# Loads of 8 KB per partition in a retention and soft-MoE kernel: one transfer per input step, weight tiles in pairs, and separate tile pools

## The chip, the cores and the metric

The kernel runs on one core of a Trainium2 chip. A core has TensorE (matmuls, and the weight loads that run beside them), VectorE (DVE), ScalarE (ACT), GpSimd (POOL) and SyncE (SP), which here issues every transfer, and 16 DMA engines that move data between HBM and the core's SBUF. The metric is the device time of one execution in microseconds; the time of the kernel before is the median of three runs.

## The reference

Retention attention over 4 batches, 8 heads, 768 positions and heads of 64, then a soft mixture of experts over all 3072 tokens. All data are float32.

```python
def _attn_ref(q, k, v):
    gamma = 1.0 - 2.0 ** (-5.0 - np.arange(H))
    for t in range(S):
        state = gamma * state + np.einsum('bhd,bhe->bhde', k[:, :, t], v[:, :, t])
        y[:, :, t] = scale * np.einsum('bhd,bhde->bhe', q[:, :, t], state)

def _moe_ref(x, phi, w1, w2):          # x: 3072 x 512, phi: 512 x 32
    logits = x @ phi
    d = softmax(logits, axis=0)
    slot_input = (d.T @ x).reshape(E, S_per_e, D)      # 8 experts, 4 slots each
    for e in range(E):                                 # w1: 512 x 1024, w2: 1024 x 512 per expert
        slot_out[e] = np.maximum(slot_input[e] @ w1[e], 0.0) @ w2[e]
    return softmax(logits, axis=1) @ slot_out
```

The second softmax over tokens needs all tokens, so no expert can start before the last token has been seen. All of w1 and w2 (32 MB) and q, k, v (k in two layouts) are read once, and 6.3 MB are written.

## The kernel before

*Retention.* The tokens are worked in 24 steps of 128 (6 per batch). Step i loads two tiles of 128 partitions by 1024 floats (4 KB per partition, 512 KB): load_kq brings k and q transposed, load_vk brings v and k in natural layout (the sixth step of a batch loads only v, 256 KB), and GpSimd scales v in place (L169). On TensorE, in this order: scores (L182), which VectorE masks (L187) into a tile A; natural (L234), which transposes the step's output before; the state's part (L202) and the scores' part (L207) of attend, scaled by VectorE into a tile x; and state (L226), copied by ScalarE. After each fourth step come logits (L245), and in the next group's first steps dispatch_p and dispatch_u (L278, L287) and combine_weights (L303).

*Experts.* After step 23 the softmaxes are closed, and hidden(g, k) multiplies the slots with w1 for expert group g (four experts each) and quarter k of the model width (L445): four weight tiles of 512 KB per call, each used in both halves of the call. hidden_t transposes the result. Then three output blocks of 256, 128 and 128 columns: 64 matmuls each with w2 (L537), group 0 first and then group 1; finish adds up the experts (L504), splits the result, and multiplies it with the combine weights (L519). VectorE and ScalarE copy each half into an output tile (L522, L525), which is written out by a transfer of 512 KB (L523). The result matmuls of a block are interleaved with the next block's matmuls. split_c and transpose_c prepare the combine weights.

*What sets the order.* TensorE runs in the order of the code. The other engines are ordered by the framework's scheduler. SyncE issues all transfers one after the other; it cannot go past one whose slot is not free. There are eight completion semaphores for transfers, used in turn, so a transfer is issued only when the one eight places ahead of it has landed.

*Tiles.* Every tile that is not small comes from one ring of 48 slots of 4 KB per partition (slot()): weights, kq and vk tiles, A, x, the combine weights, outputs.

*Weights.* load_weights(n) issues the next n tiles of a list of 64: w1 for group 0, quarters 0 to 3, then group 1, then w2 block by block. 34 tiles are spread over the 23 steps from the first (NPRE), the last two steps and the closing of the softmaxes ask for TAIL = 2, 2, 1 and 2 more, and the calls of hidden for four each.

Of the kernel before, what the change touches and what calls it, by code (L numbers as in the profile page):

```python
# [17 lines left out]
C = 128  # L18
# [6 lines left out]
NE = 8  # L25
# [52 lines left out]
def retention_soft_moe_kernel(  # L78
    ctx: ExitStack,
    tc: tile.TileContext,  # L80
    kq_in: bass.AP,
    vk_in: bass.AP,
    phi: bass.AP,
    w1: bass.AP,
    w2: bass.AP,
# [37 lines left out]
    w1t, w2t, w2n = {}, {}, [0]  # L123
    weights = [("w1", 4 * g + j, k) for g in range(2) for k in range(NK) for j in range(4)]
    for cb, (_, w) in enumerate(BLOCKS):
        for g in range(2):
            if w == 64:
                weights += [("w2", 4 * g + 2 * j, cb) for j in range(2)]
            else:
                weights += [("w2", 4 * g + j, cb) for _ in range(NFC // FPS[w]) for j in range(4)]  # L130

    def load_weights(n):
        for _ in range(n):
            if not weights:
                return
            which, e, k = weights.pop(0)
            t = slot()
            if which == "w1":
                nc.sync.dma_start(t, w1[e, k * 128:(k + 1) * 128, :])
                w1t[e, k] = t  # L140
            else:
                n = 1024 if BLOCKS[k][1] == 64 else FPS[BLOCKS[k][1]] * BLOCKS[k][1]
                nc.sync.dma_start(t[:, 0:n], w2[w2n[0]:w2n[0] + 128 * n].rearrange("(p n) -> p n", n=n))
                w2n[0] += 128 * n
                if BLOCKS[k][1] == 64:
                    w2t[e, k], w2t[e + 1, k] = [t[:, 0:512]], [t[:, 512:1024]]
                else:
                    w2t.setdefault((e, k), []).append(t)
# [3 lines left out]
    def load_kq(i):  # L152
        t = slot()
        nc.sync.dma_start(t, kq_in[i])
        st[i] = dict(kT=t[:, 0:512].rearrange("p (g t) -> p g t", t=C),
                     qT=t[:, 512:1024].rearrange("p (g t) -> p g t", t=C))

    def load_vk(i):
        t = slot()
        v = t[:, 0:512].rearrange("p (h e) -> p h e", e=D)  # L160
        st[i].update(v=v, kn=t[:, 512:1024].rearrange("p (h e) -> p h e", e=D))
        if i % NC == NC - 1:
            nc.sync.dma_start(t[:, 0:512], vk_in[i, :, 0:512])
        elif i == 0:
            nc.sync.dma_start(t[:, 0:512], vk_in[i, :, 0:512])
            nc.sync.dma_start(t[:, 512:1024], vk_in[i, :, 512:1024])
        else:
            nc.sync.dma_start(t, vk_in[i])
        nc.gpsimd.tensor_tensor(v, v, vsc[:, i % NC, :].unsqueeze(2).broadcast_to([128, H, D]), ALU.mult)  # L169

    def scores(i):
# [12 lines left out]
        A = s["A"] = slot().rearrange("p (r g t) -> p r g t", r=2, t=C)  # L184
# [133 lines left out]
    def split_c(q):  # L318
        c4s[q] = slot().rearrange("p (i r h s) -> p i r h s", r=2, h=2, s=NSLOT)
# [3 lines left out]
        nc.vector.tensor_tensor(c4r[:, :, :, 1, :], cq, c4s[q][:, :, :, 0, :], ALU.subtract)  # L323
        c4T[q] = slot()
# [12 lines left out]
    load_kq(0)  # L337
# [6 lines left out]
    load_vk(0)  # L344
    load_kq(1)
    nc.sync.dma_start(kt[:, K_FIRST:], consts[:, K_FIRST:])
    load_vk(1)
# [11 lines left out]
    for i in range(NSTEP):  # L359
# [21 lines left out]
        if i == NSTEP - 3:  # L381
            split_c(0)
        if i == NSTEP - 2:
            split_c(1)
# [6 lines left out]
        if last:  # L391
            logits(NGRP - 1)
        elif i % GRP == GRP - 1:
            logits_mm(i // GRP, range(GRP))
            logits(i // GRP)

# [68 lines left out]
    for k in range(NK):  # L465
        hidden(0, k)
        load_weights(HLOAD if k == 0 else 4)
        if k == 0:
            combine_weights(NGRP - 1)
        if k == 0:  # L470
            hT = [slot().rearrange("p (f e s) -> p f e s", e=NE, s=NSLOT) for _ in range(2)]
# [7 lines left out]
    load_weights(4)  # L479
    hidden(1, 1)  # L480
    hidden_t(0)
    load_weights(4)
# [4 lines left out]
    load_weights(4)  # L487
# [67 lines left out]
def lay_out(q, k, v, moe_phi, moe_w1, moe_w2):  # L555
# [44 lines left out]
```

## Time and profile before

| | |
|---|---|
| median of three runs | 169.55 us (169.42 to 169.83) |
| profiled execution | 170.2 us, of which the span of instructions 168.4 us |
| TensorE's granted clock, mean | 0.997 |
| busy in the span | DVE 56%, ACT 25%, POOL 18% |
| transfers | 128 by the program; 64.62 MB, mean 384 GB/s |
| HBM | 57.96 MB read, 6.29 MB written |

In the profile PE stands for TensorE's matmuls and PEld for its weight loads. The page cuts the span into 40 slices of 4.2 us and gives for each the busy share in tenths and the rate of the DMA engines. A row of instructions names its line in the kernel, the tile written and the tiles read, and the count. In the chain and in timelines the first column is the start and the second the length in us; in rows of waits stand the total, the number of times and the longest; in groups of instructions the busy time and the mean in ns, and then the idle time ahead of them with what ended it. A row of a stretch has its length, then busy time and instructions of PE, PEld, DVE, ACT and POOL, then the granted clock, the share of the DMA engines and their GB/s.

### The profile page before, as it was taken

The numbers are of one execution on the slowest core, as the hardware profiler recorded it, in microseconds if no ns is written. First come the engines' busy times: TensorE is split into PE (matmuls) and PEld (weight loads), VectorE is DVE, ScalarE is ACT, GpSimd is POOL, SyncE is SP. The second block draws the span as 40 slices with busy tenths as digits, with TensorE's granted clock in tenths as the row PEclk, the third lists the DMA queues.
The fourth block names the chain that finished last, engine by engine and source line by source line (L and its number), as shares of the span: only waits on it lengthen the run. The fifth ranks groups of instructions, "written<-read, shape, count | busy, mean of one in ns | idle before, by whom it ended". The sixth has DMA issues, their size and how long they took to land.

```text
span 168.4 us, 5648 instructions
## 1 busy us (share of the span) xinstructions
PE 153.6 (91%) x2370; PEld 109.6 (65%) x2370; DVE 93.6 (56%) x299; ACT 42.0 (25%) x104; POOL 30.5 (18%) x40
## 2 busy tenths in 40 slices
PE   8699779999999999999989799999999999999940
PEld 2577667687868786888678578867432546666620
DVE  0576445596677876694777566984223121355550
ACT  3022213232423141323212232315202030043330
POOL 0252222230304122232223221300050000000000
PEclk9999999999999999999999999999999999999998
DMA  6999999999999999999999999999999999969966
GB/s 185 324 416 411 408 402 415 401 410 406 410 407 406 407 409 406 408 409 404 407 407 411 405 409 406 403 384 367 378 312 404 415 412 406 412 263 397 384 266 263
DMA packets 18458, 64.62 MB, mean 384 GB/s; under 512 B 2048, under 2 KB 2432, under 8 KB 18432
## 3 DMA queue, kind: packets, MB, share of 16 engines
q1 hardware_dynamic: 18432, 64.26, 97.4%
q8 instruction: 19, 0.31, 0.8%
q14 instruction: 7, 0.06, 0.1%
HBM read 57.96 MB, written 6.29 MB: 381 GB/s over the span
## 4 chain that ended last, share of the span: by engine, by line
PE 50%; DMA 40%; DVE 3%; SPq 2%; issue 1%; DVEq 0%
DMA r<-in_kq_dram 18%; DMA r<-in_w_dram 18%; PE sc L537 9%; PE sc L182 6%; PE y L445 4%; PE y L207 4%; DMA r<-in_vk_dram 4%; PE xp L234 3%; PE sm L245 3%; PE y L202 3%; PE xp L445 2%; PE S L445 2%; PE sm L287 2%; PE S L226 2%; PE sm L519 2%; PE sm L331 1%
## 5 line engine op out<-in xcount | busy, mean ns | idle before, releaser
L187 DVE TENSOR_TENSOR r<-sc,kt 128x256 f32<-128x256 f32 x94 | 33.3, 417 | 17.1 <-PE sc L182 16.1
L169 POOL TENSOR_TENSOR r<-r,kt 128x512 f32<-128x512 f32 x24 | 25.1, 1044 | 75.5 <-DMA r<-in_vk_dram 51.1
L213 DVE SCALAR_TENSOR_TENSOR r<-y,kt,ysc 128x128 f32<-128x128 f32 x96 | 27.7, 343 | 9.6 <-PE y L207 6.7
L182 PE MATMUL sc<-r 64*128 64x128 f32 x376 | 27.4, 284 | 4.4 <-DMA r<-in_kq_dram 4.1
L207 PE MATMUL y<-r 128*64 128x128 f32 x384 | 27.3, 280 | 2.6 <-POOL r L169 2.4
L182 PEld LDWEIGHTS sc<-r 64*128 64x128 f32 x376 | 23.1, 187 | 7.3 <-issue 4.0
L207 PEld LDWEIGHTS y<-r 128*64 128x64 f32 x384 | 21.3, 136 | 7.3 <-POOL r L169 3.8
L235 ACT COPY r<-xp 128x512 f32<-128x512 f32 x23 | 13.5, 586 | 42.9 <-PE xp L234 33.3
L234 PE MATMUL xp<-kt,r 128*128 128x128 f32 x96 | 16.5, 287 | 0.1
L537 PE MATMUL sc<-r 128*32 128x128 f32 (+1 forms) x384 | 15.9, 310 | 0.0
L234 PEld LDWEIGHTS xp<-kt,r 128*128 128x128 f32 x96 | 10.6, 141 | 7.0 <-DVE r L187 3.4
L537 PEld LDWEIGHTS sc<-r 128*32 128x32 f32 x384 | 10.6, 110 | 6.0 <-issue 2.9
L228 ACT COPY sst<-S 128x256 f32<-128x256 f32 x20 | 7.5, 373 | 27.6 <-PE S L226 27.5
L202 PE MATMUL y<-r,sst 64*64 64x128 f32 x320 | 13.3, 282 | 0.0
L226 PE MATMUL S<-r 128*64 128x64 f32 x320 | 13.1, 222 | 0.0
L226 PEld LDWEIGHTS S<-r 128*64 128x64 f32 x320 | 12.3, 138 | 0.0
L202 PEld LDWEIGHTS y<-r,sst 64*64 64x64 f32 x320 | 8.5, 132 | 3.3 <-issue 2.1
L445 PE MATMUL y<-r,siT 128*32 128x512 f32 x64 | 8.2, 597 | 0.0
L245 PE MATMUL sm<-r,phis 128*32 128x128 f32 x192 | 7.3, 276 | 0.0
L245 PEld LDWEIGHTS sm<-r,phis 128*32 128x32 f32 x192 | 5.4, 109 | 1.4 <-issue 1.0
L313 POOL TENSOR_TENSOR cnat<-cnat,cz 128x128 f32<-128x128 f32 x6 | 2.4, 401 | 17.5 <-DVE cz L312 14.5
L287 PE MATMUL sm<-r,p 128*32 128x512 f32 x40 | 5.3, 605 | 0.0
(112 smaller groups left out, 124.2 us busy)
## 6 DMA issues: line engine op xcount, KB each, us to landing
r<-in_w_dram SPq DMA_DIRECT2D x64, 512.0 KB, 10.1
r<-in_kq_dram SPq DMA_DIRECT2D x24, 512.0 KB, 10.1
r<-in_vk_dram SPq DMA_DIRECT2D x19, 512.0 KB, 10.1
out_dram<-r SPq DMA_DIRECT2D x12, 512.0 KB, 4.3
r<-in_vk_dram SPq DMA_DIRECT2D x6, 256.0 KB, 9.6
kt<-in_consts_dram SPq DMA_DIRECT2D x1, 136.0 KB, 3.1
kt<-in_consts_dram SPq DMA_DIRECT2D x1, 78.0 KB, 5.6
phis<-in_phi_dram SPq DMA_DIRECT2D x1, 64.0 KB, 6.2
```

Source lines behind the costliest of these rows:

```text
L169: nc.gpsimd.tensor_tensor(v, v, vsc[:, i % NC, :].unsqueeze(2).broadcast_to([128, H, D]), ALU.mult)
L182: nc.tensor.matmul(sc[g // 2][r][:, g % 2, :], s["kT"][sl, g, :], s["qT"][sl, g, :], start=True, stop=True)
L187: nc.vector.tensor_tensor(A[:, r, 2 * hf:2 * hf + 2], sc[hf][r], mask.unsqueeze(1).broadcast_to([128, 2, C]), ALU.mult)
L202: nc.tensor.matmul(y[b][o:o + D, gl, :], sst[sl, g, :], s["qT"][sl, g, :], start=(gl == 0), stop=False, skip_group_check=True)
L207: nc.tensor.matmul(y[g // 2][o:o + D, g % 2, :], s["v"][:, 2 * g + r, :], s["A"][:, r, g, :], start=(c == 0 and g % 2 == 0), stop=True, sk ...
L213: nc.vector.scalar_tensor_tensor(yT[:, g, :], y[g // 2][:, g % 2, :], ybs[:, c, g:g + 1], ysc[:, g, :], ALU.mult, ALU.mult)
L226: nc.tensor.matmul(S_[r * D:(r + 1) * D, g, :], s["kn"][:, 2 * g + r, :], s["v"][:, 2 * g + r, :], start=(c == 0 and g == 0), stop=True, s ...
L234: nc.tensor.transpose(xp[:, g * 128:(g + 1) * 128], s["yT"][:, g, :], ident)
L235: (nc.vector.tensor_copy if i == NSTEP - 1 else nc.scalar.copy)(s["xn"], xp)
L245: nc.tensor.matmul(q["ltp"][32 * j:32 * j + 32, :], phis[:, p, :], st[GRP * g + j]["yT"][:, p, :], start=(p == 0), stop=(p == NPAIR - 1), ...
L445: nc.tensor.matmul(hp[g][half][32 * j:32 * j + 32, :], siT[:, k, :], w1t[4 * g + j, k][:, half * 512:(half + 1) * 512], start=(k == 0), st ...
L537: nc.tensor.matmul(op[32 * j:32 * j + 32, :w], hT[fc // 4][:, fc % 4, 4 * g + j, :], t[:, f * w:(f + 1) * w], start=(g == 0 and fc == 0), ...
```

## The change

Inputs and weights are laid out in memory so that one row of a transfer is 8 KB: x_in holds kq and vk of a step side by side, w_in holds the tiles of two experts side by side. One transfer then moves 1 MB. The amount of data and the arithmetic are the same.

- load_in replaces load_kq and load_vk: one transfer of 1 MB (768 KB in a batch's last step), issued behind state(i). Steps 0 and 1 still come in parts, as before.
- load_weights(n) issues pairs. The ring holds 17 pairs (8 KB slots), and the eighteenth pair goes as two transfers of 512 KB into two slots of the x pool.
- The one ring of 48 slots becomes four pools: the ring (17 of 8 KB), inputs (3 of 8 KB), A (2 of 4 KB), x (6 of 4 KB; outputs and other results too): 192 KB per partition, as before. The combine weights' tiles come from the input pool.
- TAIL becomes 0, 0, 1, 0 and each call in the hidden layer asks for two pairs.
- split_c(0) moves from step 21 to step 22, split_c(1) from step 22 to behind the loop.

```diff
-TAIL = (2, 2, 1, 2)
-HLOAD = 4
+TAIL = (0, 0, 1, 0)
+HLOAD = 2
-NPRE = 34
+NPRE = 17
-NRING = 48
+NRING = 17
+NIN = 3
+NX = 6
...
     ring = ctx.enter_context(tc.tile_pool(name="ring", bufs=NRING))
+    inp = ctx.enter_context(tc.tile_pool(name="inp", bufs=NIN))
+    apool = ctx.enter_context(tc.tile_pool(name="apool", bufs=2))
+    xpool = ctx.enter_context(tc.tile_pool(name="xpool", bufs=NX))
...
     def slot():
-        return ring.tile([128, 1024], F32, name="r", tag="r")
+        return xpool.tile([128, 1024], F32, name="x", tag="x")
+    def a_slot():
+        return apool.tile([128, 1024], F32, name="a", tag="a")
+    def in_slot():
+        return inp.tile([128, 2048], F32, name="in", tag="in")
...
-            t = slot()
-            if which == "w1":
-                nc.sync.dma_start(t, w1[e, k * 128:(k + 1) * 128, :])
-                w1t[e, k] = t
+            src = w_in[wn[0]]
+            wn[0] += 1
+            if nld[0] == NRING:
+                t = [slot(), slot()]
+                for h in range(2):
+                    nc.sync.dma_start(t[h], src[:, 1024 * h:1024 * h + 1024])
             else:
...
+                a = ring.tile([128, 2048], F32, name="r", tag="r")
+                nc.sync.dma_start(a, src)
+                t = [a[:, 0:1024], a[:, 1024:2048]]
+            nld[0] += 1
...
+    def load_in(i, part=None):
+        if part != 1:
+            t = in_slot()
...
+        end = 1536 if i % NC == NC - 1 else 2048
+        if part is None:
+            nc.sync.dma_start(t[:, 0:end], x_in[i, :, 0:end])
...
         attend(i)
-        if i + 2 < NSTEP:
-            load_kq(i + 2)
         state(i)
         if i + 2 < NSTEP:
-            load_vk(i + 2)
+            load_in(i + 2)
         else:
             load_weights(TAIL[i - NSTEP + 2])
...
-        if i == NSTEP - 3:
+        if i == NSTEP - 2:
             split_c(0)
-        if i == NSTEP - 2:
-            split_c(1)
...
     for k in range(NK):
         hidden(0, k)
-        load_weights(HLOAD if k == 0 else 4)
+        load_weights(HLOAD)
...
-    load_weights(4)
+    load_weights(2)
```

Two places of SyncE's program show what moves. First, the loads after the program's first eight transfers; in_kq_dram and in_vk_dram are the inputs, in_w_dram the weights, r a slot of the ring, DMAHW the completion of an earlier transfer. Before:

```order
L139 DMA r<-in_w_dram 128x1024 [waits DMAHW0_49]
L154 DMA r<-in_kq_dram 128x1024 [waits DMAHW1_49]
L168 DMA r<-in_vk_dram 128x1024 [waits DMAHW2_49]
L139 DMA r<-in_w_dram 128x1024 [waits DMAHW3_49]
L154 DMA r<-in_kq_dram 128x1024 [waits DMAHW4_49]
L168 DMA r<-in_vk_dram 128x1024 [waits DMAHW5_49]
L139 DMA r<-in_w_dram 128x1024 [waits DMAHW6_49]
L139 DMA r<-in_w_dram 128x1024 [waits DMAHW7_49]
```

And in the changed kernel (in_x_dram holds the inputs, in is a slot of the input pool):

```order
L174 DMA in<-in_x_dram 128x2048 [waits DMAHW0_49]
L152 DMA r<-in_w_dram 128x2048 [waits DMAHW1_49]
L174 DMA in<-in_x_dram 128x2048 [waits DMAHW2_49,DMAHW3_49,PE_49,Pool_49]
L152 DMA r<-in_w_dram 128x2048
L174 DMA in<-in_x_dram 128x2048 [waits DMAHW4_49,DMAHW6_49,PE_49,Pool_49]
L174 DMA in<-in_x_dram 128x1536 [waits DMAHW0_49,DMAHW5_49,PE_49,Pool_49]
L152 DMA r<-in_w_dram 128x2048
```

Input 2 now comes ahead of the first weights, and from input 3 on each input's load waits for TensorE and GpSimd to be done with the slot it takes.

Second, the end of the inputs and the weights behind them. Before, the last input's two transfers are followed by weight tiles, each of which waits for the eighth transfer ahead and for a slot that some earlier work of TensorE, VectorE, ScalarE or GpSimd leaves:

```order
L154 DMA r<-in_kq_dram 128x1024 [waits DMAHW2_49,DVE_49,PE_49]
L163 DMA r<-in_vk_dram 128x512 [waits DMAHW3_49,PE_49,Pool_49]
L143 DMA r<-in_w_dram 128x1024 [waits DMAHW4_49,PE_49,Pool_49]
L143 DMA r<-in_w_dram 128x1024 [waits DMAHW5_49,PE_49,Activation_49]
L143 DMA r<-in_w_dram 128x1024 [waits DMAHW6_49,PE_49,Activation_49]
L143 DMA r<-in_w_dram 128x1024 [waits DMAHW7_49,DVE_49,PE_49]
L143 DMA r<-in_w_dram 128x1024 [waits DMAHW0_49,PE_49,Pool_49]
```

In the changed kernel:

```order
L174 DMA in<-in_x_dram 128x1536 [waits DMAHW0_49,DMAHW5_49,PE_49,Pool_49]
L152 DMA r<-in_w_dram 128x2048
L149 DMA x<-in_w_dram 128x1024 [waits DVE_49,DMAHW7_49,PE_49,Activation_49]
L149 DMA x<-in_w_dram 128x1024 [waits DVE_49,PE_49,Activation_49]
L152 DMA r<-in_w_dram 128x2048 [waits DMAHW1_49,PE_49]
L152 DMA r<-in_w_dram 128x2048 [waits DMAHW2_49,PE_49]
L152 DMA r<-in_w_dram 128x2048 [waits DMAHW3_49,PE_49]
```

Behind the last input stand the seventeenth pair, which takes the ring's last unused slot, the eighteenth in x slots, and then pairs that take the slots of the first pairs of w1, in turn; those are read by hidden(0, 0), hidden(0, 1) and so on. The 12 output transfers stand behind the last pair on SyncE in both kernels.

More of the change, by code (lines that the diff above doesn't have):

```diff
@@ L80, in retention_soft_moe_kernel @@
     tc: tile.TileContext,
[L81 to L82 removed]
+    x_in: bass.AP,
     phi: bass.AP,
[L84 to L85 removed]
+    w_in: bass.AP,
     consts: bass.AP,
@@ L120, in retention_soft_moe_kernel @@
     ybs = kt[:, K_YB:K_YB + 24].rearrange("p (c g) -> p c g", g=NPAIR)
-    w1t, w2t, w2n = {}, {}, [0]
-    weights = [("w1", 4 * g + j, k) for g in range(2) for k in range(NK) for j in range(4)]
+    w1t, w2t, wn, nld = {}, {}, [0], [0]
+    weights = [("w1", 4 * g + 2 * j, k) for g in range(2) for k in range(NK) for j in range(2)]
     for cb, (_, w) in enumerate(BLOCKS):
         for g in range(2):
[L127 to L130, printed above, removed]
+            weights += [("w2", 4 * g + 2 * j, cb) for _ in range(NFC // FPS[w]) for j in range(2)]
     def load_weights(n):
@@ new lines, in load_weights @@
+            wn[0] += 1
[3 more added lines that the diff above has]
+                    nc.sync.dma_start(t[h], src[:, 1024 * h:1024 * h + 1024])
+            else:
+                a = ring.tile([128, 2048], F32, name="r", tag="r")
+                nc.sync.dma_start(a, src)
+                t = [a[:, 0:1024], a[:, 1024:2048]]
+            nld[0] += 1
+            for h in range(2):
+                if which == "w1":
+                    w1t[e + h, k] = t[h]
@@ L147, in load_weights @@
                 else:
-                    w2t.setdefault((e, k), []).append(t)
+                    w2t.setdefault((e + h, k), []).append(t[h])
     st = {}
[L152 to L163, printed above, removed]
+    def load_in(i, part=None):
+        if part != 1:
+            t = in_slot()
+            st[i] = dict(t=t, kT=t[:, 0:512].rearrange("p (g t) -> p g t", t=C),
+                         qT=t[:, 512:1024].rearrange("p (g t) -> p g t", t=C),
+                         v=t[:, 1024:1536].rearrange("p (h e) -> p h e", e=D),
+                         kn=t[:, 1536:2048].rearrange("p (h e) -> p h e", e=D))
+        t = st[i]["t"]
+        end = 1536 if i % NC == NC - 1 else 2048
+        if part is None:
+            nc.sync.dma_start(t[:, 0:end], x_in[i, :, 0:end])
+        elif part == 0:
+            nc.sync.dma_start(t[:, 0:1024], x_in[i, :, 0:1024])
+            return
@@ L183, in scores @@
                                  start=True, stop=True)
-        A = s["A"] = slot().rearrange("p (r g t) -> p r g t", r=2, t=C)
+        A = s["A"] = a_slot().rearrange("p (r g t) -> p r g t", r=2, t=C)
         for hf in range(2):
@@ L318, in split_c @@
     def split_c(q):
-        c4s[q] = slot().rearrange("p (i r h s) -> p i r h s", r=2, h=2, s=NSLOT)
+        t = in_slot()
+        c4s[q] = t[:, 0:1024].rearrange("p (i r h s) -> p i r h s", r=2, h=2, s=NSLOT)
         c4r = c4s[q].bitcast(F32R)
@@ L323, in split_c @@
         nc.vector.tensor_tensor(c4r[:, :, :, 1, :], cq, c4s[q][:, :, :, 0, :], ALU.subtract)
-        c4T[q] = slot()
+        c4T[q] = t[:, 1024:2048]
     c4p = {}
@@ L343, in retention_soft_moe_kernel @@
                             .broadcast_to([128, NPAIR, 16, 8]), ALU.mult)
-    load_vk(0)
-    load_kq(1)
+    load_in(0, 1)
+    load_in(1, 0)
     nc.sync.dma_start(kt[:, K_FIRST:], consts[:, K_FIRST:])
-    load_vk(1)
+    load_in(1, 1)
     nc.sync.dma_start(phis, phi)
@@ L395, in retention_soft_moe_kernel @@
             logits(i // GRP)
+    split_c(1)
     transpose_c(0, 0, "S")
@@ L470, in retention_soft_moe_kernel @@
         if k == 0:
-            hT = [slot().rearrange("p (f e s) -> p f e s", e=NE, s=NSLOT) for _ in range(2)]
+            hT = [a_slot().rearrange("p (f e s) -> p f e s", e=NE, s=NSLOT) for _ in range(2)]
             for t in hT:
```

34 lines of the change are left out of this document (13 added, 21 removed).

## Prediction

> **What bounds the kernel now.** I read the page first (busy times, the 40 slices, the queues), then the chain, the waits, the timelines of SyncE and TensorE, and the stretches around the end of the retention steps.
>
> ```profile
> PE 153.6 (91%) x2370; PEld 109.6 (65%) x2370; DVE 93.6 (56%) x299; ACT 42.0 (25%) x104; POOL 30.5 (18%) x40
> DMA  6999999999999999999999999999999999969966
> GB/s 185 324 416 411 408 402 415 401 410 406 410 407 406 407 409 406 408 409 404 407 407 411 405 409 406 403 384 367 378 312 404 415 412 406 412 263 397 384 266 263
> q1 hardware_dynamic: 18432, 64.26, 97.4%
> ```
>
> Two resources are full at once. The 16 DMA engines work for 97.4% of the span at about 407 GB/s, and TensorE is busy for 91%. So time in which the DMA engines have nothing to do is lost, and a faster DMA pays only where TensorE waits for it. Where it waits, the waits (in total, times, longest) and TensorE's timeline tell (the bracket is the idle time ahead of a row):
>
> ```profile
> PE sc L182 <- DMA r<-in_kq_dram: 4.1, 5, 1.2
> ...
> 17.89 1.16 PE L182 MATMUL sc<-r 64*128 64x128 f32 x16 [1.12 <-DMA r<-in_kq_dram]
> 23.02 1.16 PE L182 MATMUL sc<-r 64*128 64x128 f32 x16 [1.25 <-DMA r<-in_kq_dram]
> 40.28 1.16 PE L182 MATMUL sc<-r 64*128 64x128 f32 x16 [0.39 <-DMA r<-in_kq_dram]
> 75.74 1.16 PE L182 MATMUL sc<-r 64*128 64x128 f32 x16 [0.19 <-DMA r<-in_kq_dram]
> 87.62 1.09 PE L207 MATMUL y<-r 128*64 128x128 f32 x16 [0.52 <-POOL r L169]
> 94.16 1.16 PE L182 MATMUL sc<-r 64*128 64x128 f32 x16 [1.13 <-DMA r<-in_kq_dram]
> 107.83 1.16 PE L182 MATMUL sc<-r 64*128 64x128 f32 x16
> ```
>
> The row at 23.02 is the scores of step 4, that at 107.83 of step 23. Between them TensorE waits 0.39 + 0.19 + 0.52 + 1.13 = 2.2 us for inputs (the POOL row is the scaling of v, itself behind a load). That is what faster inputs can give after step 4. The chain shows the rest of the program: from 94 us on it names TensorE alone, so weights arrive in time there.
>
> ```profile
> 119.32 1.00 PE xp L445 x8
> 120.31 0.86 PE y L445 x8
> ...
> 155.17 0.43 PE y L519
> ...
> 156.06 0.79 PE sc L537 x24
> ```
>
> 119.32 is the first hidden-layer piece, hidden(0, 0), called T0 below. The row at 156.06 is a piece of output block 2; by the count of matmuls the block's second half, the first user of the last weights, begins in it, at about 156.3. The one at 155.17 is the first result matmul of block 1.
>
> How the queue lives shows in SyncE's timeline and in the times to landing:
>
> ```profile
> 4.01 0.99 SPq L348 DMA_DIRECT2D phis<-in_phi_dram  x1
> ...
> 53.31 0.33 SPq L168 DMA_DIRECT2D r<-in_vk_dram  x1
> 53.97 1.61 SPq L139 DMA_DIRECT2D r<-in_w_dram  x2
> ...
> 96.66 0.33 SPq L154 DMA_DIRECT2D r<-in_kq_dram  x1
> 97.93 0.33 SPq L163 DMA_DIRECT2D r<-in_vk_dram  x1
> 99.22 40.59 SPq L143 DMA_DIRECT2D r<-in_w_dram  x32
> ...
> 111.98 27.83 SPq L143 DMA_DIRECT2D r<-in_w_dram  x24
> 148.52 15.36 SPq L523 DMA_DIRECT2D out_dram<-r  x12
> DMA to landing us min/median/max: 3.2/10.1/11.4
> ...
> phis<-in_phi_dram SPq DMA_DIRECT2D x1, 64.0 KB, 6.2
> SPq L596 <- DMA out_dram<-r: 3.5, 3, 1.2
> out_dram<-r SPq DMA_DIRECT2D x12, 512.0 KB, 4.3
> L523 SPq DMA_DIRECT2D out_dram<-r x12: 332/332/827, 148.5 to 163.4; - x12
> ```
>
> A transfer is issued when the one eight places ahead has landed, so the spacing of issues is the time of one landing: 512 KB take 1.28 us (96.66, 97.93, 99.22), and a step's 256 KB of values alone take 0.66 us (53.31 to 53.97). Eight of them make the 10.1 us to landing. The line of landings is that of the kq loads; its least, 3.2 us, is the first load of the program, alone in the queue: 1.28 us of data and 1.9 us around it.
>
> **The change, part by part.**
>
> *Rows of 8 KB.* No row of the trace moves 8 KB per partition for data. From the two spacings: a fixed part f and d per 256 KB give f + 2d = 1.28 and f + d = 0.66, so d = 0.62, f = 0.04, and 1 MB in one transfer is f + 4d = 2.52 us against 2 x 1.28 = 2.56 now. The spacings are good to about 0.03, so f lies between 0 and 0.10 and 1 MB between 2.46 and 2.56. I take 2.52. The Trainium skill (DMA: Bandwidth & Descriptors, section "Where 436 GB/s comes from") gives the ports into SBUF 435 GB/s at most; the slices of 401 to 416 agree, and by that ceiling 1 MB could not take less than 2.41 us, an estimate from the page, which would take 1.5 us off the sum below (14 loads by 0.11) and leave its sign.
>
> *SyncE issues 75 transfers instead of 128.* At 0.33 us each, spaced by 1.28, SyncE is not what limits; I count nothing.
>
> *Start.* The first eight transfers are the same up to phis, which lands at 4.01 + 6.2 = 10.2 us. Then the queue holds input 2, a pair, input 3, a pair, input 4: 5 x 2.52 = 12.6, so input 4 lands at 22.8 and step 4 starts at 23.0 as now. The waits up to there stay; kq no longer comes ahead of vk, which is in this count.
>
> *Inputs in three slots.* The load of input i+2 now waits until state(i-1) and the scaling of v have released a slot, with the next pair queued behind it on SyncE. It is requested two steps ahead of its use, and a step is (107.83 - 23.02 - 2.2) / 19 = 4.35 us of TensorE. At worst it takes 1.9 + 2.52 + 2.52 (a pair ahead) = 6.9 of 8.7 us, so the wait is hidden; without that slack every step would pay the difference. Over the phase the engines move inputs 5 to 23 (15 whole, 4 of 768 KB, so 18) and 14 pairs: 32 x 2.52 = 80.6, input 23 at 103.4; TensorE wants it at 23.0 + 82.6 = 105.6. The margin is 2.2 us in 83, so nearly all 2.2 us of waits go; I take 2.0 (ends: 0, if the margin is eaten, and 2.2). T0 moves to 117.3. The scaling of v (1.04 us a step) ends behind the scores and transposes of the step, 1.16 + 0.66 us, and stays hidden.
>
> ```profile
> L169 POOL TENSOR_TENSOR r<-r,kt 128x512 f32<-128x512 f32 x24 | 25.1, 1044 | 75.5 <-DMA r<-in_vk_dram 51.1
> L323 DVE TENSOR_TENSOR r<-cnat,r 128x512 fp32r<-128x512 f32 x3 | 2.1, 685 | 0.0
> 118.00:123.00 5.00, 5.00 (x45) 2.18 (x48) 1.31 (x5) 1.27 (x3) 0.00 (x0) 1.00 0.98 355
> 153.00:158.00 5.00, 5.00 (x100) 3.47 (x101) 2.78 (x6) 1.82 (x5) 0.00 (x0) 1.00 1.01 397
> ```
>
> *split_c moves* by a step. The two halves on VectorE (0.7 us and less each) still stand in the last two steps; one now stands ahead of a step's masks. Between -0.7 and +0.7, one such piece hidden or exposed; I take 0, since one of them stood there before.
>
> *Separate pools, the part that decides.* Today one ring of 48 slots serves all, and as inputs end, their slots take weights: after the last input (97.93) SyncE has issued 8 weight tiles by 111.98 (32 less 24), and the row from 118 to 123 us shows the DMA engines still 98% busy, at 355 GB/s. In the changed kernel the 17 pairs of the ring are full with the hidden layer's weights and one pair of the second layer; one more pair goes into two x slots. With input 23 at 103.4 and these two pairs, the last load lands at about 103.4 + 5.1 = 108.5. The next one waits for the release of a pair by hidden(0, 0), whose two halves end at 117.3 + 1.00 + 0.86 = 119.2, and its data follow the latency. About 11 us of DMA time are lost, where today some 4 MB are moved. Then 14 pairs remain, 14 x 2.52 = 35.3 us, released faster than they are moved (two per 1.86 us). The 12 output transfers stand behind them in the same queue. The three last outputs of today land 1.2 us apart (waits of the last row of the program: at most 1.2); between that and 1.28 I take 1.25, 15.0 us for 12. From 163.4 + 4.3 = 167.7 to the span's end 168.4 it is 0.7 us.
>
> *Sum:* 119.2 + 1.9 + 35.3 = 156.4 for the last weights, + 15.0 = 171.4 for the last output, + 0.7 = 172.1. Against 168.4 that is 3.7 us more. The profiled execution took 170.2 (its span and 1.8 us around it), 0.65 above the median of 169.55; I add the difference to the median: 173.3.
>
> **The rivals.**
>
> *Outputs move beside loads* (ends on the other side: no change). If writing to HBM took nothing from reading, the outputs would not stand behind the weights, and only the landing of the last pair would count. Block 2's second half starts 156.3 - 119.3 = 37.0 after T0, which would be 154.3; the pair lands at 156.4, so TensorE loses 2.1 and has gained 2.0: 168.5, a time of 169.7. It decides when more than 3.7 of the 15 us overlap. Against it: 153 to 158 us is nearly output alone and fills the engines to 1.01 at 397 GB/s, and no slice exceeds 416. 0.05.
>
> *A large transfer is much cheaper* (faster). To come out even, 14 loads must win 3.7 us, 0.26 each: 1 MB in 2.26 us. That needs a fixed part of 0.30 per transfer, where the spacings show 0.04; the first load's 1.9 us besides data is hidden with eight in flight. By this mechanism a fixed part of 0.4 would give 2.16 us, a sum of 167.1 and a time of 168.3. The Trainium skill (DMA: Bandwidth & Descriptors, section "Bandwidth") has this as a rule that speaks for the change, to batch to 1 MB and more, with 341 GB/s at 1 MB and 425 at 16 MB. Here queued loads of 512 KB already run at 400 and more, so the trace does not agree that the size costs much. The chance is 0.05.
>
> *8 KB rows save nothing.* At 2.56 us, and 1.28 for an output, the margin of the inputs shrinks to 23.0 + 81.9 = 104.9 against 105.6, and perhaps half of the waits stay (1.1 of gain, T0 at 118.2): 118.2 + 1.9 + 1.9 + 35.8 + 15.4 + 0.7 = 173.9, a time of 175.1. The two spacings are too rough to exclude it. 0.23.
>
> *Six x slots hold up the end.* Block 1's output tiles need slots that block 0's outputs free, and those land only behind the weights, the first at 157.7. Today 7.8 us lie between the end of block 1's first result matmul (155.6) and the last output's issue, then 4.3 to landing: 157.7 + 12.1 = 169.8, under the 171.4 of the queue by 1.6. Copies that wait in line on VectorE and ScalarE and hold TensorE up by 3 us would add 1.4: 174.7. 0.10.
>
> **How the numbers follow.** The forecast as summed has 0.52; 0.05 stays for mixtures between it and today's time, 0.02 of it within 0.3%. Up to the bounds of the costs: 0 gained, 2.56 and 1.28 give 119.3 + 1.9 + 1.9 + 35.8 + 15.4 + 0.7 = 175.0, a time of 176.2; 2.2 gained, 2.46 and 1.2 give 117.1 + 3.8 + 34.4 + 14.4 + 0.7 = 170.4, a time of 171.6. The range is 170.8 to 176.0, which leaves out the first two rivals (0.10), the mixtures (0.05) and a little of each bound. Three runs differ by 0.24%, so 0.3% either way is what can be told from no change. Faster 0.05 (the cheaper transfer), the same 0.07 (outputs beside loads, and mixtures), slower 0.88 (0.52 + 0.23 + 0.10 + 0.03).
>
> **What the changed profile would show.** Right: two or three slices near 108 to 120 us with DMA far below 9, a busy queue from 121 us to the end, a last weight load landing near 156, outputs that wait many us to land, few input waits of TensorE after 23 us, hidden(0, 0) near 117.3. Wrong: no such gap (then pairs were requested earlier than I read), outputs landing while weights still move, above 430 GB/s in full slices, or input waits in most steps (then three slots are too few).

## The result and the profile after

The changed kernel takes 180.13 us (median of four runs, 178.57 to 181.96), beside 169.69 us for the kernel before on the same chip: 1.058 times as long, with a 95% interval of 1.048 to 1.068. It is slower, as predicted, but by 10.4 us where 3.7 were forecast, and outside the range. Its executions scatter by 2%. Medians here and below are over all executions, while ratios leave out those more than 1.5% above the fastest of their kernel, as the profiled one is here (181.96 us, span 180.2, against spans of 176.8 to 179.2 in the other three). By the ratio the change costs 9.8 us.

The page first: TensorE's busy time, the DMA engines by slices, their GB/s, and the program's queue.

```profile
PE 156.1 (87%) x2370; PEld 111.2 (62%) x2370; DVE 92.6 (51%) x299; ACT 42.0 (23%) x104; POOL 30.9 (17%) x40
DMA  5999999999999999999999997004999999999756
GB/s 143 319 421 418 422 420 420 387 358 402 415 416 382 418 426 420 407 386 415 373 375 418 411 376 312 6 0 124 415 429 429 415 424 416 426 368 419 306 238 263
q1 hardware_dynamic: 10800, 64.25, 88.9%
```

Full slices run at 415 to 429 GB/s, a little faster than before (about 407), and yet the queue is busy for 88.9% instead of 97.4%. Slices 25 to 28 show where: 312, 6, 0 and 124 GB/s, between 108 and 126 us. Smaller dents (387, 358, 382, 373) lie in the retention steps, and the last slices stay far below 400. A stretch shows the gap itself, from 113 to 124 us:

```profile
113.00:124.00 11.00, 10.84 (x118) 7.25 (x118) 4.42 (x16) 3.39 (x12) 0.95 (x1) 1.00 0.01 1
```

SyncE's timeline and two of its waits show it from the side of the requests:

```profile
101.16 0.33 SPq L174 DMA_DIRECT2D in<-in_x_dram  x1
101.53 0.43 SPq L152 DMA_DIRECT2D r<-in_w_dram  x1
103.51 1.02 SPq L149 DMA_DIRECT2D x<-in_w_dram  x2
123.17 18.93 SPq L152 DMA_DIRECT2D r<-in_w_dram  x14
150.82 24.71 SPq L536 DMA_DIRECT2D out_dram<-x  x12
```

```profile
SPq L174 <- PE S L241: 65.3, 18, 5.0
SPq L152 <- PE sm L318: 18.8, 1, 18.8
```

From 104.5 to 123.17 us nothing is requested: SyncE waits 18.8 us for one release by TensorE. Then 14 pairs follow. In the retention steps SyncE waits 65.3 us in all until state (L241) frees a slot for the next input, with the weight pairs queued behind it. Next, the steps on TensorE (timeline, idle time in the bracket) and three rows of the waits:

```profile
24.95 1.16 PE L197 MATMUL sc<-in 64*128 64x128 f32 x16 [1.14 <-DMA in<-in_x_dram]
59.42 1.16 PE L197 MATMUL sc<-in 64*128 64x128 f32 x16 [0.42 <-DMA in<-in_x_dram]
121.22 1.06 PE L458 MATMUL xp<-r,siT 128*32 128x512 f32 x8
164.87 0.76 PE L532 MATMUL y<-in,x 128*128 128x512 f32 x1 [5.77 <-DVE x L520]
```

```profile
PE sc L197 <- DMA in<-in_x_dram: 7.4, 7, 2.2
DVE x L519 <- DMA out_dram<-x: 6.7, 1, 6.7
PE y L532 <- DVE x L520: 5.8, 1, 5.8
```

The first hidden piece (T0) starts at 121.2 us, after 119.3 before and 117.3 in the forecast. The waits of the scores for inputs rose from 4.1 to 7.4 us instead of vanishing. Behind step 4, where the forecast had 2.0 of 2.2 us of waits go, they came to 3.4 (the waits from 25.5 to 116 us):

```profile
PE sc L197 <- DMA in<-in_x_dram: 3.4, 4, 1.2
```

Near the end, block 1's result matmuls wait 5.77 us because VectorE waits 6.7 us for an output to land and free an x slot.

The last view is of single lines: the input loads from 30 to 110 us, the first pair behind the gap, and the last pair. Under each instruction row stands the time from issue to landing.

```profile
L174 SPq DMA_DIRECT2D in<-in_x_dram x17: 327/328/328, 29.9 to 101.2; - x17
DMA to landing us min/median/max: 6.6/7.4/9.3
...
L152 SPq DMA_DIRECT2D r<-in_w_dram x1: 328/328/328, 123.2 to 123.2; - x1
DMA to landing us min/median/max: 6.1/6.1/6.1
...
L152 SPq DMA_DIRECT2D r<-in_w_dram x1: 328/328/328, 141.8 to 141.8; - x1
DMA to landing us min/median/max: 20.9/20.9/20.9
```

An input took at least 6.6 us, where the prediction had 6.9 as the worst case. The first pair behind the gap landed at 123.2 + 6.1 = 129.3, the last at 141.8 + 20.9 = 162.7 (forecast 156.4).

### The profile page after: what moved, and what is told of

Its sections match the earlier page's. It is cut to its first block, busy times and chain, and to the rows that moved or that the text cites. A ratio compares the mean times of both kernels' runs of the same rounds, so it can differ in the third digit from the quotient of the medians.

```text
span 180.2 us, 5555 instructions
## 1 busy us (share of the span) xinstructions
PE 156.1 (87%) x2370; PEld 111.2 (62%) x2370; DVE 92.6 (51%) x299; ACT 42.0 (23%) x104; POOL 30.9 (17%) x40
## 3 DMA queue, kind: packets, MB, share of 16 engines
q1 hardware_dynamic: 10800, 64.25, 88.9%
## 4 chain that ended last, share of the span: by engine, by line
PE 56%; DMA 31%; DVE 4%; issue 2%; POOL 1%; SPq 1%; ACT 1%; DVEq 0%; POOLq 0%
DMA in<-in_x_dram 24%; PE y L222 9%; PE sc L197 7%; DMA out_dram<-x 7%; PE sc L550 7%; PE xp L249 4%; PE y L458 4%; PE sm L260 4%; PE y L217 3%; PE S L241 3%; PE sm L302 3%; PE xp L458 2%; PE S L458 2%; PE sm L347 1%; PE sm L532 1%
## 5 line engine op out<-in xcount | busy, mean ns | idle before, releaser
L202 DVE TENSOR_TENSOR a<-sc,kt 128x256 f32<-128x256 f32 x94 | 33.4, 417 | 20.2 <-PE sc L197 20.2
L184 POOL TENSOR_TENSOR in<-in,kt 128x512 f32<-128x512 f32 x24 | 25.0, 1043 | 75.4 <-DMA in<-in_x_dram 61.4
L197 PE MATMUL sc<-in 64*128 64x128 f32 x376 | 27.4, 284 | 7.5 <-DMA in<-in_x_dram 7.4
L228 DVE SCALAR_TENSOR_TENSOR x<-y,kt,ysc 128x128 f32<-128x128 f32 x96 | 28.2, 344 | 11.1 <-PE y L222 7.9
L197 PEld LDWEIGHTS sc<-in 64*128 64x128 f32 x376 | 23.1, 187 | 10.9 <-issue 6.5
L222 PE MATMUL y<-a,in 128*64 128x128 f32 x384 | 27.6, 279 | 1.7 <-POOL in L184 1.4
L222 PEld LDWEIGHTS y<-a,in 128*64 128x64 f32 x384 | 21.6, 136 | 6.2 <-issue 3.6
L250 ACT COPY x<-xp 128x512 f32<-128x512 f32 x23 | 13.5, 586 | 44.7 <-PE xp L249 44.7
L550 PE MATMUL sc<-r,a 128*32 128x128 f32 (+1 forms) x368 | 17.5, 317 | 1.0 <-DMA r<-in_w_dram 1.0
L550 PEld LDWEIGHTS sc<-r,a 128*32 128x32 f32 x368 | 11.3, 113 | 8.0 <-issue 3.3
L249 PE MATMUL xp<-kt,x 128*128 128x128 f32 x96 | 15.5, 284 | 0.0
L241 PE MATMUL S<-in 128*64 128x64 f32 x320 | 13.1, 223 | 0.0
L241 PEld LDWEIGHTS S<-in 128*64 128x64 f32 x320 | 12.2, 138 | 0.1
```

The lines of the kernel that those rows point to most:

```text
L197: nc.tensor.matmul(sc[g // 2][r][:, g % 2, :], s["kT"][sl, g, :], s["qT"][sl, g, :], start=True, stop=True)
L202: nc.vector.tensor_tensor(A[:, r, 2 * hf:2 * hf + 2], sc[hf][r], mask.unsqueeze(1).broadcast_to([128, 2, C]), ALU.mult)
L222: nc.tensor.matmul(y[g // 2][o:o + D, g % 2, :], s["v"][:, 2 * g + r, :], s["A"][:, r, g, :], start=(c == 0 and g % 2 == 0), stop=True, sk ...
L228: nc.vector.scalar_tensor_tensor(yT[:, g, :], y[g // 2][:, g % 2, :], ybs[:, c, g:g + 1], ysc[:, g, :], ALU.mult, ALU.mult)
L241: nc.tensor.matmul(S_[r * D:(r + 1) * D, g, :], s["kn"][:, 2 * g + r, :], s["v"][:, 2 * g + r, :], start=(c == 0 and g == 0), stop=True, s ...
L249: nc.tensor.transpose(xp[:, g * 128:(g + 1) * 128], s["yT"][:, g, :], ident)
```

## The experiments

Theory: the pools cost the time. Tiles that lie unused in one pool are room that the weights lack, so the queue runs dry from the last input to T0; and three input slots and six x slots add waits of their own. Rival: the transfers of 8 KB rows themselves cost it. Comparisons are with the kernel before on the same chip.

### One pool with 8 KB rows

```diff
-NRING = 17
-NIN = 3
-NX = 6
+NRING = 23
-TAIL = (0, 0, 1, 0)
+TAIL = (1, 1, 1, 1)
     def slot():
-        return xpool.tile([128, 1024], F32, name="x", tag="x")
+        if not halves:
+            t = in_slot()               # a slot of the ring, 8 KB
+            halves.extend([t[:, 0:1024], t[:, 1024:2048]])
+        return halves.pop(0)
```

> One ring of 23 slots of 8 KB in place of the ring of 17, the input pool and the x pool (A keeps its two slots); 8 KB rows, 1 MB transfers and the 17 pairs spread over the steps as in the changed kernel; the tail may ask for one pair in each of the last two steps and twice while the softmaxes close. Theory 'pools' (the fixed pools leave the DMA engines without a free slot before the hidden layer, and inputs without one in the steps): the gap before the hidden layer goes, the last weights land near 150 us, and the time falls to 168 to 171 us (ratio 0.99 to 1.01). Theory 'rows' (a transfer of 1 MB lands too late, whatever the pools): the waits of TensorE for inputs stay at 7 us and the time at 176 or more.

Measured: 169.51 us, ratio 1.001 (0.999 to 1.004). The whole loss is gone with the 1 MB transfers left in, so the rival falls. TensorE's timeline at T0; then, by their lines, the input loads from 30 us on, and the pairs requested from T0 on:

```profile
118.80 1.06 PE L453 MATMUL xp<-r,siT 128*32 128x512 f32 x8
```

```profile
L169 SPq DMA_DIRECT2D r<-in_x_dram x13: 327/328/328, 33.9 to 92.9; - x13
DMA to landing us min/median/max: 12.8/19.3/20.7
...
L148 SPq DMA_DIRECT2D r<-in_w_dram x11: 327/328/1332, 120.8 to 133.3; - x11
```

With shared slots an input is requested some 19 us ahead instead of 7, and only 11 pairs are left to be requested from T0 on instead of 14.

### One more pair ahead of T0

```diff
-                a = ring.tile([128, 2048], F32, name="r", tag="r")
+                a = in_slot() if nld[0] == NRING + 1 else ring.tile([128, 2048], F32, name="r", tag="r")
-TAIL = (0, 0, 1, 0)
+TAIL = (0, 0, 1, 1)
     def split_c(q):
-        t = in_slot()
+        t = ring.tile([128, 2048], F32, name="r", tag="r") if q == 2 else in_slot()
```

> The changed kernel with one more pair of weights, the nineteenth, loaded into a slot of the input pool before the hidden layer; the last combine-weight tile moves to a ring slot instead. Theory 'pools': one pair of 2.5 us moves from behind the gap into it, so the time falls by about 2.5 us, to 177.6. Rival 'x slots' (the end is set by output tiles waiting for slots, not by the queue of loads): less than 1 us.

Measured: 179.51 us, ratio 1.054 (1.048 to 1.061): 0.6 us less than the changed kernel by the medians, where 2.5 were expected, and inside its scatter. By itself this run is inconclusive. Its profile (span 175.8) is more useful: T0 at 119.35, and the extra pair lands alone.

```profile
L152 SPq DMA_DIRECT2D in<-in_w_dram x1: 328/328/328, 112.2 to 112.2; - x1
DMA to landing us min/median/max: 4.8/4.8/4.8
...
L152 SPq DMA_DIRECT2D r<-in_w_dram x13: 327/328/1260, 121.3 to 137.3; - x13
```

A lone 1 MB transfer takes 4.8 us from issue to landing, 2.3 more than the 2.5 of its data.

### Outputs from the ring instead of the x slots

```diff
-                ot = slot()
+                ot = ring.tile([128, 2048], F32, name="r", tag="r")[:, 0:1024]
-        s4 = slot()
+        s4 = ring.tile([128, 2048], F32, name="r", tag="r")[:, 0:1024]
```

> The changed kernel with its output tiles taken from the ring (free at the end) instead of the six x slots. Theory 'pools' with the queue of loads as the limit: the 12 outputs still stand behind the last weights; only the 1.3 us that the last three come late are won, and up to 1 us of slower clock: 178 to 179.5. Rival 'x slots': TensorE's wait of 5.8 us on the output slots was the limit, and the time falls by 4 us or more.

Measured: 181.04 us, ratio 1.056 (1.052 to 1.059), no gain. But the profiled run (span 181.3) shows that the end did get shorter: T0 came at 124.27, 3 us later than in the changed kernel's, and the span grew by only 1.1. T0 was late for longer waits for inputs (6.5 us behind step 4 instead of 3.4), which the edit does not touch. By the completion events the last output landed 15.0 us behind the last pair, 16.5 in the changed kernel. The first row below is T0 on TensorE's timeline. In the stretches at its end (the row is length, busy of PE, PEld, DVE, ACT and POOL, clock, DMA share, GB/s) the queue stays full:

```profile
124.27 1.07 PE L458 MATMUL xp<-r,siT 128*32 128x512 f32 x8
```

```profile
160.00:170.00 10.00, 7.06 (x137) 4.82 (x129) 3.71 (x9) 2.07 (x4) 0.00 (x0) 1.00 1.01 401
170.00:180.00 10.00, 1.73 (x6) 0.99 (x6) 1.89 (x3) 1.65 (x3) 0.00 (x0) 0.75 0.85 349
```

### Four input slots, sixteen pairs in the ring

```diff
-NPRE = 17
-NRING = 17
-NIN = 3
+NPRE = 16
+NRING = 16
+NIN = 4
```

> The changed kernel with four input slots instead of three, and the 8 KB taken from the ring (16 pairs, 16 of them in the steps, the seventeenth in x slots). If three slots make the inputs late, TensorE's waits for inputs fall from 7.4 us to under 4 and the hidden layer begins 2 to 4 us sooner; the pair fewer before the gap costs 2.5 us at the end, so the time stays within 178 to 181. If the inputs are late for another reason (the weights ahead of them in the queue, the slowest of the 16 engines), the waits stay at 6 to 8 us and the time rises by 2 us.

Measured: 180.93 us, ratio 1.065 (1.061 to 1.069). The trade is even, and the profile shows both sides of it: the wait of the scores, T0 on the timeline, and the loads by line (inputs, then pairs from T0 on).

```profile
PE sc L197 <- DMA in<-in_x_dram: 1.4, 2, 1.1
```

```profile
118.28 1.06 PE L458 MATMUL xp<-r,siT 128*32 128x512 f32 x8
```

```profile
L174 SPq DMA_DIRECT2D in<-in_x_dram x16: 327/328/331, 30.8 to 93.4; - x16
DMA to landing us min/median/max: 9.0/10.0/11.1
...
L152 SPq DMA_DIRECT2D r<-in_w_dram x15: 327/328/1495, 120.2 to 141.3; - x15
```

Inputs are requested a step earlier (10.0 us to landing instead of 7.4), the waits of the scores fall from 7.4 to 1.4 us (behind step 4 from 3.4 to none), and T0 comes 2.9 us sooner. But 15 pairs remain instead of 14, 2.5 us more, and the gap comes earlier without getting shorter: by the packets of the trace it lies from 109.0 to 121.2 us instead of 112.9 to 124.1.

### Two pairs behind the last inputs

```diff
-TAIL = (0, 0, 1, 0)
-NPRE = 17
+TAIL = (1, 1, 1, 0)
+NPRE = 15
```

> The changed kernel, with two of its 17 early weight pairs loaded behind the inputs of the retention steps instead of between them (one behind each of the last two requests for inputs). Pools, slots, rows, number of transfers and what is left for the end (14 pairs) stay. Theory 'lead': TensorE waits for inputs because a load that is requested two steps ahead still finds a pair of 2.48 us ahead of it; with fewer pairs among the inputs the first hidden piece starts near 116 to 117 us instead of 121.3, the input waits of TensorE fall from 7.4 us to under 3, the gap in the DMA stays, and the time is 116.5 + 1.9 + 6.1 + 13 x 2.49 + 15.0 + 1.5 + 0.7 + 1.8 = 175.9, so 174 to 177.5. Theory 'slots': three input slots are released too late whatever else is in the queue; the waits stay above 5 us, the first hidden piece stays near 120 to 121 us, and the time is 179 to 181.

Measured: 180.51 us, ratio 1.055 (1.047 to 1.063): the theory "lead" is wrong here. The waits of the scores fell to 3.0 us, near what it said, but T0 stayed at 120.82, as the rival said. Inputs still took 7.0 to 9.9 us to land. All of the 3.0 us lie behind step 4, where the changed kernel has 3.4, so two pairs fewer among the inputs changed little there. What went are the waits up to step 4, in a start in which TensorE itself was slow: the clock was low from 8 to 14 us, 0.53 in the last row below (a stretch, its clock ahead of the DMA share; above it the wait and T0).

```profile
PE sc L197 <- DMA in<-in_x_dram: 3.0, 4, 1.3
```

```profile
120.82 1.06 PE L458 MATMUL xp<-r,siT 128*32 128x512 f32 x8
```

```profile
8.00:14.00 6.00, 4.85 (x49) 4.50 (x50) 1.22 (x4) 0.37 (x1) 3.23 (x6) 0.53 1.02 397
```

That start did not hold T0 back against the changed kernel: step 4's scores began at 24.65 us, 0.3 earlier, and from there to T0 it took 96.2 us in this run and 96.3 in the changed kernel.

### The changed kernel with 4 KB rows

```diff
-                nc.sync.dma_start(a, src)
+                nc.sync.dma_start(a[:, 0:1024], src[:, 0:1024])
+                nc.sync.dma_start(a[:, 1024:2048], src[:, 1024:2048])
-            nc.sync.dma_start(t[:, 0:end], x_in[i, :, 0:end])
+            nc.sync.dma_start(t[:, 0:1024], x_in[i, :, 0:1024])
+            nc.sync.dma_start(t[:, 1024:end], x_in[i, :, 1024:end])
```

> The changed kernel with every 1 MB transfer issued as two of 512 KB with 4 KB per partition; pools, slots and the order stay. If rows of 8 KB cost time here (one landing of 1 MB that has to wait for the slowest of the 16 DMA engines), this is faster by 2 us or more: under 178. If they save time (1 MB in 2.48 us against 2 x 1.28), the 14 pairs at the end cost 14 x 0.08 = 1.1 us more and the inputs come later: 181 to 184. If the size of the transfer does not matter and the pools alone make the difference: 179 to 181.5, with the same gap of 14 to 16 us between two landings around 120 us.

Measured: 183.43 us (180.99 to 186.57), ratio 1.068 (1.063 to 1.074): by the ratios 1%, or 1.7 us, above the changed kernel, with intervals that touch (the medians lie 3.3 us apart). T0 was 122.71. Rows of 8 KB do not cost time here; if anything they save some.

### The order: fewer pairs among the inputs, in both good kernels

```diff
 # one pool                  # the kernel before
-TAIL = (1, 1, 1, 1)        -TAIL = (2, 2, 1, 2)
-NPRE = 17                  -NPRE = 34
+TAIL = (1, 1, 1, 2)        +TAIL = (2, 2, 2, 4)
+NPRE = 15                  +NPRE = 30
```

> One ring of 23 slots of 8 KB for everything (it took 169.51 us), with 15 instead of 17 pairs among the inputs; the other two follow behind them. Theory 'lead': here too the inputs wait behind weights, so the first hidden piece moves from 118.8 to about 115.5 to 116.5, weights and outputs follow it, and the time falls by 2.5 to 4 us: 165.5 to 167. Theory 'slots': with 23 shared slots no input is late for want of a slot, so nothing is won: 169 to 170.

> The kernel before, with 30 instead of 34 weight tiles among the inputs and the other four behind them; its ring, tiles and rows of 4 KB stay. Theory 'lead': the first hidden piece moves from 119.3 to about 115.5 to 116.5 and the time falls to 166 to 167.5. If rows of 8 KB matter by themselves at a good order, the ring of 8 KB with 15 early pairs beats this by 0.5% or more; if they do not, the two agree within 0.5%. If the order does not matter: 169 to 170.

Measured: 166.67 us, ratio 0.982 (0.979 to 0.985), and 166.96 us, ratio 0.983 (0.980 to 0.986). Both beat both kernels of this study. Their T0 came 3.5 and 4.4 us sooner (TensorE's timeline of one pool with 15 early pairs, then of the kernel before with 30 early tiles):

```profile
115.32 1.07 PE L453 MATMUL xp<-r,siT 128*32 128x512 f32 x8
```

```profile
114.83 1.06 PE L445 MATMUL xp<-r,siT 128*32 128x512 f32 x8
```

About 2 us of each gain lie ahead of step 4, whose scores began at 22.94 us instead of 24.96 in one pool (where the clock was 0.66 from 20 to 25 us) and at 21.16 instead of 23.02 in the kernel before. Behind step 4 the waits for inputs, 1.4 and 2.2 us, went. Where the slots let inputs be requested far ahead, weights moved behind them pay; in the changed kernel, whose lead is set by three slots, the same edit paid nothing.

### One separation at a time

```diff
 # sep_in: inputs and split_c's tiles apart     # sep_x: x, s4 and outputs apart
-NRING = 23                                     -NRING = 23
+NRING = 20                                     +NRING = 20
+NIN = 3                                        +NX = 6
-            t = in_slot()                      -TAIL = (1, 1, 1, 1)
+            t = inp.tile(...)                  +TAIL = (0, 0, 0, 1)
```

> The one-pool kernel (169.51 us) with one of the three separations put back: the inputs (and split_c's tiles at the end) have three slots of their own, and pairs, x and outputs share a ring of 20. Theory 'gap' (the changed kernel loses its time because the DMA engines have no free room from the last input on): 21 pairs are still requested before the first hidden piece, so the gap is as short as in the one-pool kernel, and only the later inputs cost, 121.3 - 118.8 = 2.5 us at most: 169.5 to 172.5. Theory 'late inputs' (three slots are what costs): 177 to 180, as the changed kernel.

> The one-pool kernel with the other separation put back: x, scores of the experts and outputs have six half slots of their own, and inputs, pairs and split_c's tiles share a ring of 20, which holds 18 pairs before the first hidden piece instead of 21. Theory 'gap': inputs come as early as in the one-pool kernel (first hidden piece at 118.8), but the DMA engines stand still from about 110 to 123 us and 14 pairs remain: 118.8 + 1.9 + 6.1 + 13 x 2.49 + 15.0 + 1.5 + 0.7 + 1.8 = 178.2, so 176 to 180. Theory 'late inputs': most of the loss is gone: 169.5 to 173.

Measured: inputs apart 175.12 us, ratio 1.032 (1.028 to 1.036); x apart 179.93 us, ratio 1.057 (1.053 to 1.062). The second is as "gap" said, the first lies between the two theories: I had counted 21 early pairs, but three slots that inputs no longer use are three that weights cannot have. Stretches with an idle queue and the pairs requested from T0 on show it, first with x apart, then with the inputs apart:

```profile
108.00:112.00 4.00, 3.78 (x61) 2.99 (x60) 3.83 (x13) 0.79 (x2) 1.74 (x3) 1.00 0.02 6
117.00:121.00 4.00, 4.00 (x36) 2.35 (x34) 0.65 (x3) 0.67 (x2) 0.00 (x0) 1.00 0.00 0
```

```profile
L145 SPq DMA_DIRECT2D r<-in_w_dram x14: 327/328/868, 120.9 to 139.5; - x14
```

```profile
112.00:117.00 5.00, 4.83 (x66) 3.61 (x63) 2.91 (x11) 2.04 (x7) 0.95 (x1) 1.00 0.01 3
```

```profile
L150 SPq DMA_DIRECT2D r<-in_w_dram x12: 327/345/1901, 122.0 to 136.8; - x12
```

The x slots are the dearer separation: with them apart the queue stands still twice and 14 pairs remain from T0 on; with the inputs apart it stands still once, and 12 remain.

### Row size alone, at the best order

```diff
-            nc.sync.dma_start(a, src)
+            nc.sync.dma_start(a[:, 0:1024], src[:, 0:1024])
+            nc.sync.dma_start(a[:, 1024:2048], src[:, 1024:2048])
-            nc.sync.dma_start(t[:, 0:end], x_in[i, :, 0:end])
+            nc.sync.dma_start(t[:, 0:1024], x_in[i, :, 0:1024])
+            nc.sync.dma_start(t[:, 1024:end], x_in[i, :, 1024:end])
```

> The fastest kernel so far (one ring of 8 KB slots, 15 early pairs, 166.67 us, ratio 0.982) with each 1 MB transfer issued as two of 512 KB with 4 KB per partition, so that only the row size differs. If rows of 8 KB are worth their 3% per landing (2.48 against 2 x 1.28 us) where the DMA engines are the bound, 32 pairs and 18 inputs cost 50 x 0.08 = 4 us more, of which at least the part behind the first hidden piece (11 to 14 pairs, about 1 us) shows: 167.5 to 170.5. If the time goes by TensorE, which is busy for 92% there, it is the same within 0.3%: 166.2 to 167.2.

Measured: 169.05 us, ratio 0.997 (0.995 to 0.999), against 0.982 with 8 KB rows: the larger rows are worth 1.5%, about 2.4 us, in this kernel. The edit also halves the size of a transfer, and with it what the eight semaphores let SyncE have under way, so the length of the row is not told apart from these. The page's rates, for 8 KB and then 4 KB rows:

```profile
GB/s 135 342 406 423 427 416 422 411 423 415 427 413 416 425 417 421 413 419 423 411 419 423 417 415 423 367 244 230 417 389 425 423 429 417 417 412 407 422 335 221
```

```profile
GB/s 136 320 358 415 415 403 409 404 409 408 406 407 404 410 405 409 406 407 405 405 408 406 410 406 406 408 377 299 334 398 418 409 406 408 406 408 412 418 422 170
```

Full slices move 411 to 427 GB/s against 403 to 415, some 3%. Both dip at slices 27 to 28, where room for weights runs short. The kernel before with 30 early tiles has 4 KB rows too and is faster by 2 us; its ring frees room in pieces of 4 KB. So in a ring of 8 KB slots the gain of the rows is about eaten by the coarser slots, which is why one pool came out even with the kernel before. That last step is an inference from these pairs of runs; no run had 8 KB rows with 4 KB slots.

## Why the prediction was wrong in size

One relation ties the profiles together. From the start of T0 to the end of the span, less 2.49 us for each pair over 14 that is requested after T0 (2.49 is the usual spacing of two landings, from the completion events of the trace), for the kernels with 8 KB rows:

| kernel | T0 | pairs | span | span - T0 - 2.49 x (pairs - 14) |
|---|---|---|---|---|
| changed kernel | 121.2 | 14 | 180.2 | 59.0 |
| one more pair early | 119.4 | 13 | 175.8 | 58.9 |
| four input slots | 118.3 | 15 | 179.5 | 58.7 |
| two pairs late | 120.8 | 14 | 180.1 | 59.3 |
| x apart | 119.0 | 14 | 178.0 | 59.0 |
| outputs from the ring | 124.3 | 14 | 181.3 | 57.0 |
| inputs apart | 120.1 | 12 | 173.2 | 58.1 |
| one pool | 118.8 | 11 | 168.0 | 56.7 |
| one pool, 15 early | 115.3 | 11 | 165.0 | 57.2 |

So the sum of the forecast has the right terms: the time is T0, plus a fixed latency, plus the pairs that found no room ahead of T0, plus the outputs behind them. The five kernels with outputs in six x slots lie at 58.7 to 59.3, the others at 56.7 to 58.1. The difference lies at the end: by the completion events the last output lands 16.4 to 16.8 us behind the last pair in the five and 15.0 to 15.2 in the others, so the x slots cost 1.2 to 1.8 us there. In time the run with outputs from the ring does not show it (1.056 against 1.058); its executions scatter by more. The changed kernel with 4 KB rows, at 184.8 - 122.7 = 62.1, does not fit: its pairs took 1.0 us longer and its outputs 2.3.

The scatter of T0 is mostly that of the waits for inputs. In the changed kernel and the runs with one more pair early, outputs from the ring, two pairs late and four input slots, these waits behind step 4 are 3.4, 2.3, 6.5, 3.0 and 0 us, and the time from step 4 to T0 less them is 92.4 to 93.2 us in all five. The scatter of the times can be read as the same (T0 from 119.4 to 124.3 us in the four with three input slots), though the runs without a profile don't show theirs.

Point by point against the sum of 172.1, whose profile came to 180.2:

- *Start: step 4's scores at 23.0.* They began at 24.95, 1.9 late: input 4 landed at 24.8 instead of 22.8. By the completion events phis landed at 11.3 us instead of 10.2, and the first pair came 3.6 us behind the transfer ahead of it instead of 2.5.
- *Inputs in three slots: "so the wait is hidden".* This step failed. From step 4 to T0 it took 96.3 us instead of 94.3: none of the waits that were to go went, and those for inputs rose from 2.2 to 3.4. The lead was worked out from a mean step (2 x 4.35 = 8.7 us), and the load from the latency of the program's first load, alone in the queue (1.9 + 2.52 + 2.52 = 6.9). The waits fall in the cheap steps, and the loads took 7.4 us in the middle and up to 9.3. Input 12 was requested at 51.90 (the chain of waits has it as 7.38 us of DMA) and wanted 7.1 us later; TensorE waited for it 0.42 us. A fourth slot took the waits behind step 4 to none. The lower end of the gain was set at 0, and nothing in the range stood for a loss.
- *The gap.* Right in cause and size, and late only as inputs and T0 were: the DMA engines stand idle for 11.2 us, from 112.9 to 124.1, where about 11 were forecast from 108.5 on, and one request waits for hidden(0, 0).
- *Restart: "the latency" of 1.9 us.* Mis-sized. From T0 to the first landed pair it took 129.3 - 121.2 = 8.1 us, forecast 1.9 + 1.9 + 2.52 = 6.3. The first pair behind the gap took 6.1 us to land, where 1.9 + 2.52 = 4.4 were counted; a lone one took 4.8.
- *The remaining pairs.* 13 spacings took 162.7 - 129.3 = 33.4 us, forecast 32.8.
- *The outputs and the end.* 180.2 - 162.7 = 17.5 us, forecast 15.7. "Six x slots hold up the end" was given 0.10 as a rival, in which it replaced the forecast; it is a term that came on top. Its price of 1.4 us was right (1.2 to 1.8).

These five differences are 1.9, 2.0, 1.8, 0.6 and 1.8, together 8.1. The other three executions had spans 1.0 to 3.4 us shorter; which of the five was smaller in them no profile shows. One reading of the prediction needs a correction: from 94 us on the chain names VectorE too (105.2 to 109.3 us, and at the end), but no transfer, so what was concluded from it holds. Of the other rivals, "8 KB rows save nothing" is wrong (3% per transfer at full slices), "outputs move beside loads" found nothing for it (the first output landed at 164.0 us, behind the last pair), and "a large transfer is much cheaper" is wrong too: from 2.56 to 2.48 us. The Trainium skill (Perfetto Trace Analysis, section "DMA Optimizations") says that batching small transfers into larger ones, from 2 KB to 4 or 8 KB, can improve throughput dramatically. No run here has 2 KB; between 4 and 8 KB per partition the gain is 3%, worth 1.5% in time where the queue is kept full.

## What to carry to other kernels

A shared ring hands the room of a finished phase to the next one; before splitting it, count for each pool the bytes that will lie unused while the next phase's loads could have been requested, and price each such MB as a transfer, and the gap besides as the latency of one restart. For a load that must be requested just in time, take the lead from the cheapest steps and the latency from loads in the same state of the queue, and let the range hold a loss as well as a gain. When inputs and weights share a queue and the slots allow a long lead, try the weights a little later: two pairs moved behind the inputs were worth 1.8%, more than the whole change of transfer size.

## What was not expected of the hardware

- *Time to land on an empty queue.* 4.8 us for 1 MB alone, and 6.0 to 6.2 us for the first pair from T0 on in six runs (the changed kernel, one more pair early, four input slots, outputs from the ring, two pairs late, x apart), where the data take 2.5. By the completion events 15 of the 16 engines finished that pair 4.7 to 4.9 us after its request, and one 1.1 to 1.4 us later. One candidate is in the page: the instruction queue's 18 packets, which take 0.6% of 16 engines' 180 us, so about 1 us each, on some engine.

```profile
q8 instruction: 18, 0.29, 0.6%
```

In each of the six one such packet falls between request and landing. The first row below is the instruction queue from 123.2 to 129.3 us in the changed kernel. With the inputs apart no such packet falls into the landing of the first pair behind the gap: the 16 engines finished it within 0.3 us, and it landed after 4.7 us, with a second pair right behind it (last two rows).

```profile
q8 instruction: 1, 0.02, 1.0%
...
L150 SPq DMA_DIRECT2D r<-in_w_dram x1: 328/328/328, 117.4 to 117.4; - x1
DMA to landing us min/median/max: 4.7/4.7/4.7
```

So the traces agree with the candidate. On which engine a packet ran they don't show, and no run changed the instruction traffic.

- *The clock behind a wait.* After the wait of 5.77 us in the changed kernel, TensorE's granted clock was 0.58 for the 7 us from 163 to 170:

```profile
163.00:170.00 7.00, 5.13 (x58) 3.43 (x62) 2.63 (x5) 1.76 (x3) 0.00 (x0) 0.58 0.87 355
```

The work behind the stall was slower too: a piece of 24 matmuls of L550 took 1.51 us at 166.41 and 0.86 at 153.45. In the run with outputs from the ring, without that wait, the clock stayed at 1.00 to 170 us. The Trainium skill (TensorE: Matmul & The Clock Gate, section "HAM oscillation — how this bites in real kernels") has this rule, with gaps of over about 3.4 us; the wait of 5.77 us agrees. But low clocks also followed shorter waits, as the one at 8 to 14 us above, in a start whose longest wait was 2.9 us (the row below), while the clock stayed at 1.00 behind one of 2.7 us in the start of the run with the inputs apart:

```profile
PE y L222 <- POOL in L184: 2.9, 1, 2.9
```
